# Gate and up with x stationary and the weights moving, in a two-layer GQA decode and SwiGLU kernel

## The chip, the cores and the metric

The kernel runs on one core of a Trainium2 chip. Its time is the device time of one execution, in microseconds; a profiled execution also gives a span, from the first to the last instruction, and a trace. Five engines take part: TensorE (PE; its weight loads are shown apart as PEld), VectorE (DVE), ScalarE (ACT), GpSimd (POOL) and SyncE (SP), which here issues every DMA.

## The reference

Two layers, run one after the other on the same weights. `x` is 4 rows (the batch) of 512; each layer is attention against a cache of 8192 keys and values, then a SwiGLU feed-forward:

```python
def _A_ref(x, k_cache, v_cache, wq, wo):      # 32 query heads, 8 key heads, Dh = 128
    q = (x @ wq).reshape(B, Sq, Hq, Dh).transpose(0, 2, 1, 3)
    scores = jnp.einsum("bhqd,bhkd->bhqk", q, k) * (Dh ** -0.5)
    o = jnp.einsum("bhqk,bhkd->bhqd", softmax(scores), v)
    return o.transpose(0, 2, 1, 3).reshape(B, Sq, Hq * Dh) @ wo

def _B_ref(x, w_gate, w_up, w_down):          # 512 -> 1792 -> 512
    g = _silu(x @ w_gate)
    u = x @ w_up
    return (g * u) @ w_down

for _ in range(2):
    x = x + _A_ref(_layernorm(x), A_k_cache, A_v_cache, A_wq, A_wo)
    x = x + _B_ref(_layernorm(x), B_w_gate, B_w_up, B_w_down)
```

All inputs are bfloat16. Keys and values are 4 x 8 x 8192 x 128 elements each, 64 MB each, and are read once per layer but for a few tiles that stay on the chip; w_gate, w_up and w_down have 1.8 MB each.

## The kernel before

**Slots and loads.** Keys and values come in tiles of 4 MB (one batch row, two key heads), 128 partitions of 32 KB. They go round through four slots of SBUF, with a fifth for wq and later for keys. A list `cmds` holds all loads in order; `pump` issues the next one on SP's queue as soon as the half-blocks that it writes are in `free`, and `freed` marks them free when the code reaches the last reader. SP itself then waits for that reader's semaphore. So the order of loads is fixed, and a late reader holds up every load behind it on that queue.

**Attention.** A tile of keys is turned in place on VectorE (L558), scores are matmuls with the keys moving (L582), the exponential is on ScalarE (L629), P is turned on VectorE (L646), and P times V runs in four quarters of the array: four matmuls with 32 stationary columns and 512 moving columns, each writing its own 32 PSUM partitions (L718). `gather`, `combine`, `mix` and `out_proj` bring the result back to `xT`, x with its 512 features over partitions.

**Feed-forward** (`ffn`, L943). `center` makes `xn`, the centred x, and the row sums for the variance; `deviation` (L901) is called after gate's second part and makes `rstd` with a matmul (L903) and two ScalarE operations. Gate and up (L961) hold a 128x128 block of the weight stationary and move the 4 columns of `xn` for one block of 128 features, 14 blocks by 4 contraction steps, for gate and up: 112 matmuls. The result has features over partitions, 14 groups of 4 batch columns, in one PSUM bank each for gate (`gb`) and up (`ub`). VectorE and ScalarE make `hT` from it in seven operations (L975 to L982). Parts of gate free space in layer 0: behind `wg0`, `wg1` and `wg2` come three loads of w_down, behind `wg3`, up and the w_down groups come loads of the next layer's first keys.

**w_down.** In layer 0 a 128x128 block of w_down is stationary and `hT` moves (L999), in five loads' order; in layer 1 `hT` is stationary, w_down moves 128 columns, and four quarters of the array make the four output parts (L989). `x_rows` (L879) has put x there before. The end is four small copies (L1062, L1064) and the store (L1066). All of w_up but 256 columns' worth of its last step lies in SBUF for both layers; w_gate, that rest and w_down are loaded again in layer 1, at the end of the queue. The last load, `W+`, waits until the last P has its place.

**Which feature on which partition.** The loads of w_down put e neighbouring rows on a partition (`WDS`, third number: 2 or 4), within a block of rows; `base` and `columns` pick the same features from w_gate and w_up by a stepped read, so that `hT` and w_down agree. `load_wd` is at L462.

Of the kernel before, what the change touches and what calls it, by code (L numbers as in the profile page):

```python
# [6 lines left out]
ALU = mybir.AluOpType  # L7
# [96 lines left out]
def bass_interleave_layers__gqa_block_cached__swiglu_ffn__decode_kernel(  # L104
# [12 lines left out]
    B, _, D = A_x.shape  # L117
    _, G, S, Dh = A_k_cache.shape
    HqDh = A_wq.shape[1]
    Hq = HqDh // Dh  # L120
    F = B_w_gate.shape[1]
    REP = Hq // G
    P = 128
    assert Dh == P and B * Hq == P and D % P == 0 and F % P == 0 and B == 4 and G % 2 == 0
    KT = D // P
    FO = F // P
# [5 lines left out]
    QB = 32  # L132
    NA = P // QB
# [7 lines left out]
    NSLOT = 4  # L141
# [3 lines left out]
    with ExitStack() as es:  # L145
        sb = lambda name, shape, dt: es.enter_context(nc.sbuf_tensor(name, shape, dt))

        SL = TT * Dh
# [3 lines left out]
        RES = FR * F + FY  # L152
        assert KT * HqDh == SL
        QS = NSLOT
        kvf = sb("kvf", [P, (NSLOT + 1) * SL + RES], BF16)
# [1 line left out]
        wq_sb = kv[:, QS, :].rearrange("p (k f) -> p k f", k=KT)  # L157
        WQ = [f"wq{i}" for i in range(NB)]
        wo_sb = sb("wo_sb", [P, Hq, D], BF16)
        WDS = (((12, 14, 2), (10, 12, 2), (0, 2, 2), (2, 6, 4), (6, 10, 4)), ((0, 8, 2), (8, 12, 2), (12, 14, 2)))  # L160
        NW = max(len(w) for w in WDS)

        W_SLOT = (1, 3)
        O_WU = KT * F
# [19 lines left out]
        def columns(o, e=2):  # L184
            return kvf[:, o:o + e * (P - 1) + 1:e]

        def base(L, fo):
            a, _, e = next(w for w in WDS[L] if w[0] <= fo < w[1])
            return a * P + (fo - a) // e * e * P + (fo - a) % e, e

        def wg_at(s, k, f, e):
            return columns(s * SL + k * F + f, e)

        def wu_at(s, k, f, e):
            o = k * F + f
            return columns((NSLOT + 1) * SL + o if o < RES else s * SL + O_WU + o - RES, e)

        def wd_at(s, fo, k):
            o = pick2(k).start
# [30 lines left out]
        own, rstd = tiny[:, 7:7 + QH], tiny[:, 7 + QH:7 + QH + B]  # L230
# [4 lines left out]
        xn = sb("xn", [P, XB], BF16)  # L235
# [9 lines left out]
        pb = sb("pb", [P, SW], BF16)  # L245
        pbf = pb[:].bitcast(FP32)
        acc = pbf[:, 0:Dh]
        n = FO * B
        gr, eg, gw = (pbf[:, i * n:(i + 1) * n] for i in range(3))
        hT = pb[:, 6 * n:7 * n]  # L250
# [23 lines left out]
        def bank(k):  # L274
            return ps[:, k * BANKF:(k + 1) * BANKF]
# [17 lines left out]
        def quarter(j):  # L293
# [7 lines left out]
        sem_w = {n: [sem(f"sem_{n}{i}") for i in range(c)]  # L301
                 for n, c in (("wq", 2), ("wo", 4), ("wg", 1), ("wu", 3), ("wd", NW))}
# [3 lines left out]
        def part_sem():  # L306
# [4 lines left out]
        T = _Sync(engines, prog)  # L311
# [6 lines left out]
             reads=["ident"], writes=["ident"])  # L318
        T.op("pool", lambda e: e.memset(quad[:], 0.0), writes=["quad"])
        for a in range(NA):  # L320
# [11 lines left out]
             reads=["ident"], writes=["head"])  # L332
# [3 lines left out]
             reads=["ident"], writes=["made"])  # L336
        T.op("dve", lambda e: e.tensor_reduce(sel[:].rearrange("p (h r) -> p h r", h=2),
                                              made.rearrange("p (h q r) -> p h r q", h=2, q=QH), AX.X, ALU.max),
             reads=["made"], writes=["sel"])
        T.op("dve", lambda e: e.tensor_reduce(own[:], made.rearrange("p (h q r) -> p q h r", h=2, q=QH),  # L340
                                              AX.XY, ALU.max),
             reads=["made"], writes=["own"])
# [46 lines left out]
        s = W_SLOT[0]  # L389
# [10 lines left out]
        n = NB - PARK  # L400
# [59 lines left out]
                    load_wd(w0, i, j)  # L460

        def load_wd(w0, L, j, also=()):  # L462
            a, b, e_ = WDS[L][j]
            o = 0 if w0 is pTf else wd_from(L, a)
            T.dma("sp", w0[:, o:o + (b - a) * D].rearrange("p (m x) -> p m x", x=e_ * D),
                  B_w_down[a * P:b * P, :].rearrange("(m p e) n -> p m (e n)", p=P, e=e_), sem_w["wd"][j],
                  writes=[f"wd{j}"] + list(also))

        def pump(most=len(cmds)):
# [34 lines left out]
        def freed(s, a, b):  # L504
            free.update((s, h) for h in halves(a, b))
            pump()
# [436 lines left out]
        def ffn(L):  # L943
            s = W_SLOT[L]
            gb, ub = OBK[0], SBK[0]
            gT = bank(gb)[:, 0:FO * B]
            uT = bank(ub)[:, 0:FO * B]
            fb = lambda ap: ap.rearrange("p (f b) -> p f b", b=B)
            rb = rstd[:].unsqueeze(1).to_broadcast([P, FO, B])
            rooms = {"wg0": room(s, 0, F), "wg1": room(s, F, 2 * F), "wg2": room(s, 2 * F, 3 * F), "wg3": room(s, 3 * F, O_WU), "wu0": [], "wu1": room(s, O_WU, O_WD)}  # L950
            for j, (a, b, _) in enumerate(WDS[L]):
                o = wd_from(L, a)
                rooms[f"wd{j}"] = ["pT"] if not L and a == FO_P else room(s, o, o + (b - a) * D)
            names = {"wg0": ["wg0"], "wg1": ["wg1"], "wg2": ["wg2"], "wg3": ["wg3"], "wu0": ["wu0"], "wu1": ["wu1", "wu2"]}
            for at, wname, bk, ks in ((wg_at, "wg0", gb, (0, 1)), (wg_at, "wg1", gb, (1, 2)),
                                      (wg_at, "wg2", gb, (2, 3)), (wg_at, "wg3", gb, (3, KT)),
                                      (wu_at, "wu0", ub, (0, KT // 2)), (wu_at, "wu1", ub, (KT // 2, KT))):
                for fo in range(FO):
                    f = base(L, fo)
                    for kt in range(*ks):  # L960
                        T.op("pe", lambda e: e.matmul(bank(bk)[:, fo * B:(fo + 1) * B],  # L961
                                                      lhsT=at(s, kt, *f),
                                                      rhs=xn[:, kt * B:(kt + 1) * B],
                                                      start=(kt == 0 and fo == 0), stop=(kt == KT - 1 and fo == FO - 1)),
                             reads=rooms[wname] + names[wname] + ["xn"], writes=[f"pb{bk}"],
                             sig=(fo == FO - 1 and kt == ks[1] - 1))
                if wname in ("wg0", "wg1", "wg2"):
                    k = int(wname[2])
                    if not L:
                        freed(s, NB + 2 + k, NB + 3 + k)  # L970
                    if k == 1:
                        deviation(zero_sb, "zero")
                elif wname != "wu0":
                    freed(s, *((0 if L else GATE, UP) if wname == "wg3" else (UP, DOWN)))
            T.op("dve", lambda e: e.tensor_tensor(fb(gr), fb(gT), rb, ALU.mult),  # L975
                 reads=[f"pb{gb}", "rstd"], writes=["gr", "pb"])
            T.op("act", lambda e: e.activation(eg, gr, ACTF.Exp, scale=-1.0), reads=["gr"], writes=["eg"])
            T.op("dve", lambda e: e.tensor_tensor(fb(gw), fb(gr), rb, ALU.mult), reads=["gr", "rstd"], writes=["gw"])
            T.op("dve", lambda e: e.tensor_scalar(eg, eg, 1.0, None, op0=ALU.add), reads=["eg"], writes=["eg"])
            T.op("dve", lambda e: e.reciprocal(eg, eg), reads=["eg"], writes=["eg"])  # L980
            T.op("dve", lambda e: e.tensor_tensor(eg, gw, eg, ALU.mult), reads=["gw", "eg"], writes=["eg"])
            T.op("dve", lambda e: e.tensor_tensor(hT, eg, uT, ALU.mult), reads=[f"pb{ub}", "eg"], writes=["hT"])  # L982
            if L == 1:
                x_rows(1)
                for i, (a, b, _) in enumerate(WDS[1]):
                    for fo in range(a, b):
                        for j in range(NA):
                            o = s * SL + O_WD + fo * D + j * P
                            T.op("pe", lambda e: e.matmul(quarter(j), lhsT=hT[:, fo * B:(fo + 1) * B],  # L989
                                                          rhs=kvf[:, o:o + P], start=False, stop=(fo == FO - 1)),  # L990
                                 reads=["hT", f"wd{i}"] + rooms[f"wd{i}"], writes=[f"part{j}"],
                                 sig=(fo == b - 1))
                freed(s, DOWN, NB)
                return
            for j, (a, b, _) in enumerate(WDS[0]):
                k = OBK[0] if j > WP else SBK[1]
                for nt in range(KT):
                    for fo in range(a, b):
                        T.op("pe", lambda e: e.matmul(bank(k)[:, nt * B:(nt + 1) * B],  # L999
                                                      lhsT=wd_at(s, fo, nt),  # L1000
                                                      rhs=hT[:, fo * B:(fo + 1) * B],
                                                      start=(j in (0, WP + 1) and nt == 0 and fo == a),
                                                      stop=(j in (WP, len(WDS[0]) - 1) and nt == KT - 1 and fo == b - 1)),
                             reads=["hT", f"wd{j}"] + rooms[f"wd{j}"], writes=[f"pb{k}"], sig=(fo == b - 1))
                if j == LATE[0]:
                    freed(s, DOWN, PARK)
                if j == len(WDS[0]) - 2:
                    freed(s, 0, MID)
                if j == WP:
                    add_to_x(bank(k)[:, 0:XB], f"pb{k}")  # L1010
                    freed(s, NB + 5, NB + 6)
            freed(s, MID, GATE)
            add_to_x(bank(k)[:, 0:XB], f"pb{k}")
# [82 lines left out]
```

## Time and profile before

| what | value |
|---|---|
| runs, median (lowest to highest) | 645.25 us (644.95 to 645.78) |
| profiled execution, its own time | 645.21 us |
| its span | 643.4 us |
| mean granted TensorE clock | 0.83 |
| PE / PEld / DVE / ACT / POOL busy | 65% / 28% / 66% / 7% / 2% of the span |
| DMA queue of the kernel | 271.33 MB, 99.0% of 16 engines |
| L961 (gate and up) | 224 matmuls, 7.0 us busy |
| L989 (w_down, layer 1) | 56 matmuls, 2.0 us busy |
| L999 (w_down, layer 0) | 56 matmuls, 2.3 us busy |

Busy time is a sum over the whole span; the bracket behind a row tells how long its engine was idle before it and what ended the wait. The chain of work that ended last is put down to the DMA for 61% of the span, to VectorE for 19% and to TensorE for 15%. A row "128\*4 128x128" is a matmul with 128 rows and 4 columns stationary, and 128 columns moving.

### The profile page before, as it was taken

The page shows a single profiled execution, that of the slowest core. Times are in us where ns is not written, and L with a number is a line of the kernel's source. Part 1 is how long each engine was busy: PE and PEld are TensorE (multiplying, and loading weights), DVE is VectorE, ACT ScalarE, POOL GpSimd, SP SyncE. Part 2 cuts the span into 40 slices and gives each one's busy share as a digit, 9 for nine tenths or more (in the row PEclk, how much of TensorE's full clock was granted, in tenths as well). Part 3 has the DMA queues.
Part 4 walks back from the last instruction along what each step waited for, and adds up shares of the span by engine and source line. Part 5 has one row for each costly group of instructions (what it writes and reads, how often), then busy time and mean ns, then how long its engine had stood idle before and what let it go on. Part 6 is the DMA issues. An engine that isn't in the chain of part 4 may idle for free.

```text
span 643.4 us, 7434 instructions
## 1 busy us (share of the span) xinstructions
PE 416.7 (65%) x3126; PEld 180.0 (28%) x3128; DVE 421.7 (66%) x593; ACT 42.3 (7%) x118; POOL 11.6 (2%) x44
## 2 busy tenths in 40 slices
PE   0673376456765757757866977776555577557877
PEld 0421122112222322222226432332221232222324
DVE  5275467455776656776952688887765567755964
ACT  0000000000000000000010110000000000000110
POOL 0000000000000000000000000000000000000000
PEclk9995786698877889766975899999778887769877
DMA  9999999999999999999999999999999999999996
GB/s 372 442 424 416 430 444 426 431 424 429 438 436 423 428 433 439 426 426 431 440 406 380 416 431 431 436 429 425 432 435 432 427 430 438 429 428 429 440 408 257
DMA packets 15872, 271.79 MB, mean 422 GB/s; under 512 B 1624, under 2 KB 1632, under 8 KB 7264
## 3 DMA queue, kind: packets, MB, share of 16 engines
q1 hardware_dynamic: 15840, 271.33, 99.0%
q8 instruction: 24, 0.39, 0.2%
q14 instruction: 8, 0.07, 0.0%
HBM read 271.32 MB, written 0.00 MB: 422 GB/s over the span
## 4 chain that ended last, share of the span: by engine, by line
DMA 61%; DVE 19%; PE 15%; issue 3%; another core or an unknown queue 1%; SPq 0%; DVEq 0%
DMA kvf<-in_A_k_cache_dram 49%; DVE kvf L558 15%; DMA kvf<-in_A_v_cache_dram 11%; PE ps L582 9%; PE ps L718 2%; DVE pb L770 2%; DMA kvf<-in_B_w_down_dram 1%; PE ps L961 1%; PE ps L917 1%; DVE pb L766 0%; DVE pT L646 0%; DVE scr L780 0%; SPq L93 0%; PE ps L861 0%
## 5 line engine op out<-in xcount | busy, mean ns | idle before, releaser
L582 PE MATMUL ps<-kvf,zq 128*128 128x512 bf16 x1024 | 292.9, 432 | 183.5 <-DVE kvf L558 178.8
L558 DVE STREAM_TRANSPOSE kvf<-kvf 128x2048 f32<-128x2048 f32 (+1 forms) x133 | 280.5, 2132 | 128.4 <-DMA kvf<-in_A_k_cache_dram 128.0
L582 PEld LDWEIGHTS ps<-kvf,zq 128*128 128x128 bf16 x1024 | 99.1, 108 | 340.2 <-DVE kvf L558 222.6
L718 PE MATMUL ps<-kvf,pT 128*32 128x512 bf16 x960 | 67.6, 405 | 1.1 <-DVE pT L646 1.1
L629 ACT ACTIVATE pb<-ps,tiny 128x512 bf16<-128x512 f32 x32 | 22.0, 687 | 525.9 <-DVE tiny L627 505.1
L646 DVE STREAM_TRANSPOSE pT<-pb 64x512 bf16<-64x512 bf16 x60 | 41.2, 686 | 2.7 <-ACT pb L629 1.7
L770 DVE SCALAR_TENSOR_TENSOR pb<-ps,tiny,pb 128x128 f32<-128x128 f32 x104 | 36.5, 351 | 4.7 <-PE ps L718 0.8
L588 DVE TENSOR_REDUCE tiny<-ps 128x1 f32<-128x512 f32 x32 | 22.0, 687 | 20.1 <-PE ps L582 20.1
L718 PEld LDWEIGHTS ps<-kvf,pT 128*32 128x32 bf16 x960 | 21.0, 99 | 31.2 <-issue 16.0
L775 PEld LDWEIGHTS ps<-sel,pb 128*128 128x128 f32 x64 | 17.0, 273 | 16.5 <-DVE pb L770 8.3
L572 POOL TENSOR_TENSOR zq<-scr,tiny 128x64 bf16<-128x64 bf16 x30 | 9.0, 299 | 527.1 <-PE ps L582 527.1
L596 DVE TENSOR_REDUCE mrm<-ps 1x8 f32<-1x128 f32 x32 | 8.8, 275 | 13.6 <-PE ps L593 13.6
L775 PE MATMUL ps<-sel,pb 128*128 128x8 f32 x64 | 12.4, 267 | 5.8 <-DVE pb L770 5.8
L619 PEld LDWEIGHTS ps<-mrm,tiny 128*128 128x128 f32 x60 | 13.0, 223 | 9.2 <-DVE scr L780 3.2
L917 PE MATMUL ps<-xn,kvf 128*128 128x4 bf16 x256 | 7.5, 166 | 11.5 <-DMA kvf<-in_A_wq_dram 11.2
L766 DVE TENSOR_SCALAR pb<-ps,tiny 128x128 f32<-128x128 f32 x32 | 10.1, 315 | 3.0 <-PE ps L718 3.0
L619 PE MATMUL ps<-mrm,tiny 128*128 128x16 f32 x60 | 9.9, 241 | 3.1 <-ACT mrm L631 3.1
L836 PE MATMUL ps<-wo_sb,scr 128*4 128x512 bf16 x48 | 11.0, 379 | 0.5 <-DVE scr L805 0.5
L917 PEld LDWEIGHTS ps<-xn,kvf 128*128 128x128 bf16 x256 | 7.3, 105 | 11.8 <-DMA kvf<-in_A_wq_dram 11.4
L631 ACT ACTIVATE mrm<-head,tiny 128x8 f32<-128x8 f32 x32 | 9.6, 301 | 1.0
L593 PE MATMUL ps<-identf,tiny 128*1 128x128 f32 x32 | 8.7, 273 | 0.7 <-DVE tiny L588 0.7
L790 DVE TENSOR_TENSOR xT<-xT,ps 128x16 f32<-128x16 f32 x6 | 1.0, 171 | 10.4 <-PE ps L846 4.7
(87 smaller groups left out, 120.3 us busy)
## 6 DMA issues: line engine op xcount, KB each, us to landing
kvf<-in_A_k_cache_dram SPq DMA_DIRECT2D x27, 4096.0 KB, 31.2
kvf<-in_A_v_cache_dram SPq DMA_DIRECT2D x27, 4096.0 KB, 33.9
kvf<-in_A_v_cache_dram SPq DMA_DIRECT2D x3, 2048.0 KB, 25.2
kvf<-in_A_k_cache_dram SPq DMA_DIRECT2D x9, 512.0 KB, 7.9
kvf<-in_A_k_cache_dram SPq DMA_DIRECT2D x2, 2048.0 KB, 9.4
kvf<-in_A_wq_dram SPq DMA_DIRECT2D x2, 2048.0 KB, 18.1
wo_sb<-in_A_wo_dram SPq DMA_DIRECT2D x4, 1024.0 KB, 41.4
kvf<-in_B_w_gate_dram SPq DMA_DIRECT2D x2, 1792.0 KB, 23.9
```

What stands on the lines that cost most here:

```text
L558: T.op("dve", lambda e: e.transpose(w, w), reads=names, writes=names)
L582: T.op("pe", lambda e: e.matmul(bank(bk)[:, 0:SW], lhsT=zq[:, z0:z0 + P], rhs=w[:, :, c // 2, :, c % 2], start=(q == 0 and c == 0), stop=( ...
L588: T.op("dve", lambda e: e.tensor_reduce(mx[:], bank(bk)[:, 0:SW], AX.X, ALU.max), reads=[f"pb{bk}"], writes=["mx"])
L619: T.op("pe", lambda e: e.matmul(at, lhsT=ones, rhs=mrm[:, i * H2:(i + 2) * H2], start=True, stop=True), reads=[f"m8{i}", "rsm", "onesf"], ...
L629: T.op("act", lambda e: e.activation(pb[:], bank(bk)[:, 0:SW], ACTF.Exp, bias=nm, accum_out=rs), reads=[f"pb{bk}", "nm"], writes=PB + ["rs"])
L646: T.op("dve", lambda e: e.transpose(dst, pb[hp]), reads=["pb", "row"], writes=[name])
L718: T.op("pe", lambda e: e.matmul(bank(k)[j * QB:(j + 1) * QB, q0 * Dh:q1 * Dh], lhsT=p_t[:, t, h, :], rhs=v[:, q0:q1, t, :], start=((last o ...
L766: T.op("dve", lambda e: e.tensor_scalar(into, o, own[:, q:q + 1], None, op0=ALU.mult), reads=[f"pb{k}", "own"], writes=["row"] if last els ...
L770: T.op("dve", lambda e: e.scalar_tensor_tensor(into, o, own[:, q:q + 1], into, op0=ALU.mult, op1=ALU.add), reads=[f"pb{k}", "own", iname], ...
L775: T.op("pe", lambda e: e.matmul(at, lhsT=into, rhs=sel[:], start=True, stop=True), reads=[iname, "sel"], writes=[name])
L836: T.op("pe", lambda e: e.matmul(bank(OUTB)[0:B, 0:D], lhsT=oT[:, h, :], rhs=wo_sb[:, h, :], start=(gp == groups[L][0] and r == 0), stop=(g ...
L917: T.op("pe", lambda e: e.matmul(at[:, h * B:(h + 1) * B], lhsT=wq_sb[:, kt, h * Dh:(h + 1) * Dh], rhs=xn[:, kt * B:(kt + 1) * B], start=(k ...
```

## The change

Three things change together, in both layers. Gate and up hold `xn` (4 columns) stationary and move the weight, 448 features in each quarter of the array: quarter a computes features 448a to 448a + 447, and its 4 result rows lie on partitions 32a to 32a + 3. That is 16 matmuls for gate and 17 for up, where one strip is cut at the edge of the resident part of w_up. `on_end` then turns each bank in place on VectorE, in 32x32 blocks that step over 14 features, so that feature 14p + f comes to partition p, at column b * 14 + f. The elementwise steps use that order; the last one writes `hT` back in (f, b) order. And w_down is loaded so that partition p holds rows 14p to 14p + 13: a load takes some of these 14 from every partition. The groups of w_down, their number and their order stay.

```diff
-        WDS = (((12, 14, 2), (10, 12, 2), (0, 2, 2), (2, 6, 4), (6, 10, 4)), ((0, 8, 2), (8, 12, 2), (12, 14, 2)))
+        WDS = (((12, 14), (10, 12), (0, 2), (2, 6), (6, 10)), ((0, 8), (8, 12), (12, 14)))
...
+        FW = F // NA
+        def wg_at(s, k, f, n):
+            o = s * SL + k * F + f
+            return kvf[:, o:o + n]
...
+        def strips(up, k):
+            for a in range(NA):
+                cuts = [a * FW, (a + 1) * FW]
+                if up and cuts[0] < RES - k * F < cuts[1]:
+                    cuts.insert(1, RES - k * F)
+                for f, end in zip(cuts, cuts[1:]):
+                    yield a, f, end - f
...
-            T.dma("sp", w0[:, o:o + (b - a) * D].rearrange("p (m x) -> p m x", x=e_ * D),
-                  B_w_down[a * P:b * P, :].rearrange("(m p e) n -> p m (e n)", p=P, e=e_), sem_w["wd"][j],
+            T.dma("sp", w0[:, o:o + (b - a) * D], B_w_down.rearrange("(p f) n -> p (f n)", f=FO)[:, a * D:b * D], sem_w["wd"][j],
...
+            def on_end(k):
+                blk = bank(k)[:, 0:FW].rearrange("p (i f) -> p f i", f=FO)
+                T.op("dve", lambda e: e.transpose(blk, blk), reads=[f"pb{k}"], writes=[f"pb{k}"])
...
-                for fo in range(FO):
-                    f = base(L, fo)
-                    for kt in range(*ks):
-                        T.op("pe", lambda e: e.matmul(bank(bk)[:, fo * B:(fo + 1) * B],
-                                                      lhsT=at(s, kt, *f),
-                                                      rhs=xn[:, kt * B:(kt + 1) * B],
-                                                      start=(kt == 0 and fo == 0), stop=(kt == KT - 1 and fo == FO - 1)),
+                for kt in range(*ks):
+                    parts = list(strips(bk == ub, kt))
+                    for n, (a, f, w) in enumerate(parts):
+                        T.op("pe", lambda e: e.matmul(bank(bk)[a * QB:a * QB + B, f - a * FW:f - a * FW + w],
+                                                      lhsT=xn[:, kt * B:(kt + 1) * B], rhs=at(s, kt, f, w),
+                                                      start=(kt == 0), stop=(kt == KT - 1)),
...
+            on_end(gb)
             T.op("dve", lambda e: e.tensor_tensor(fb(gr), fb(gT), rb, ALU.mult),
...
-            T.op("dve", lambda e: e.tensor_tensor(hT, eg, uT, ALU.mult), reads=[f"pb{ub}", "eg"], writes=["hT"])
+            on_end(ub)
+            T.op("dve", lambda e: e.tensor_tensor(hT.rearrange("p (f b) -> p b f", b=B), fb(eg), fb(uT), ALU.mult), reads=[f"pb{ub}", "eg"], writes=["hT"])
```

## The prediction

> **What bounds the kernel now.** I read the page, then the last 10 us in order of time, then busy time and clock by stretch, and last the same work in layer 0. The page first:
>
> ```profile
> DMA  9999999999999999999999999999999999999996
> GB/s 372 442 424 416 430 444 426 431 424 429 438 436 423 428 433 439 426 426 431 440 406 380 416 431 431 436 429 425 432 435 432 427 430 438 429 428 429 440 408 257
> ...
> q1 hardware_dynamic: 15840, 271.33, 99.0%
> ```
>
> The DMA engines are busy nearly always, so elsewhere a faster engine only waits longer for data. Two dips are to be seen: slices 21 and 22 (322 to 354 us), where layer 0 ends, and the last slice. The change touches just these: the loads around layer 0's feed-forward, and the chain that ends the kernel. That end in order of time (start, duration, engine, line):
>
> ```profile
> 635.46 0.84 PE L961 MATMUL ps<-xn,kvf 128*128 128x4 bf16 x28
> 636.13 0.30 PEld L903 LDWEIGHTS ps<-pb,tiny 128*128 128x128 f32 x2
> 636.16 0.36 PE L903 MATMUL ps<-pb,tiny 128*128 128x4 f32 x2
> 636.38 2.36 PE L961 MATMUL ps<-xn,kvf 128*128 128x4 bf16 x84
> ...
> 637.28 0.22 DVE L975 TENSOR_TENSOR pb<-ps,tiny 128x56 f32<-128x56 f32 x1 [1.47 <-PE ps L961]
> ...
> 638.58 0.22 DVE L981 TENSOR_TENSOR pb<-pb 128x56 f32<-128x56 f32 x1
> 638.90 0.21 DVE L982 TENSOR_TENSOR pb<-pb,ps 128x56 bf16<-128x56 f32 x1
> 639.16 0.74 PEld L989 LDWEIGHTS ps<-kvf,pb 128*4 128x4 bf16 x32 [0.19 <-DVE pb L982]
> ...
> 640.15 0.31 PEld L989 LDWEIGHTS ps<-kvf,pb 128*4 128x4 bf16 x16 [0.25 <-DMA kvf<-in_B_w_down_dram]
> 640.78 0.10 PEld L989 LDWEIGHTS ps<-kvf,pb 128*4 128x4 bf16 x8 [0.32 <-DMA kvf<-in_B_w_down_dram]
> 641.19 0.60 DVE L1064 CAST pb<-ps 4x128 bf16<-4x128 f32 x2 [2.08 <-PE ps L989]
> ```
>
> Two chains meet here. One is arithmetic: gate and up, SiLU on VectorE, w_down. The other is the last loads of w_down: PE twice stops for them, and the last 8 matmuls run at 640.78 because the data came then. So there is slack ahead of w_down: its 56 matmuls take less than the 2.0 us between 639.17 and 641.16. Clock and DMA in the stretches between the instants at which the clock changed:
>
> ```profile
> 629.91:633.32 3.41, 2.43 (x47) 1.21 (x41) 2.03 (x7) 0.00 (x0) 0.00 (x0) 1.00 1.01 403
> 633.32:636.74 3.42, 3.14 (x88) 2.67 (x89) 0.96 (x6) 0.18 (x1) 0.00 (x0) 1.00 0.95 354
> 636.74:640.15 3.41, 3.41 (x116) 2.95 (x112) 1.56 (x6) 0.63 (x3) 0.00 (x0) 0.50 0.37 138
> ```
>
> TensorE loses half its clock at 636.74 (third number from the end) although PE counts as fully busy: 4 moving columns a matmul are hardly any streaming.
>
> **The change part by part.**
>
> *Gate and up on TensorE.* 112 matmuls a layer (four moving columns, 28 in 0.84 us at full clock, 84 in 2.36 us mostly at half) give way to 33 with 448 moving columns (one strip is cut into 192 and 256), in four quarters. The nearest row is L718, which also writes quarters: 16 of 512 columns in 1.05 us at full clock, 24 in 2.75 us at half. With 0.38 us for the last one's own duration that is 0.22 us per round of four at full clock and 0.46 at half; for 448 columns 0.2 and 0.4. Layer 1: gate's first two rounds let the variance matmul L903 start at 635.9, where its input (L898) is ready, and not at 636.13. The deviation then comes 0.25 us sooner; gate ends at 636.7.
>
> *Two transposes a layer on VectorE.* Each is 128x448 float32 in PSUM, in place, stepping 14 elements. Rows: L558 takes 1215 ns for 1024 and 2294 ns for 2048, so 136 ns and 1.054 ns an element: 0.61 us. L521 and L524, with PSUM on one side, take 1224 and 1236 ns for 1024, the same. Bounds: 0.47 us (no fixed part), and 1.08 us if every stepped element takes two turns. I take 0.61, since L926 reads PSUM in steps of 4 elements and takes 291 ns for 128, on the unstepped rate; no row shows a stepped write. The first transpose starts at 636.73 and ends at 637.34. It covers the wait for the deviation and delays L975 from 637.28 to 637.37: +0.09. Behind it the chain to L981's end is as before. The second transpose stands alone between L981 and the last multiply, since up has long ended: 0.61 + 0.03. The last multiply writes hT in steps of 4; I cost that at nothing, as L926's stepped reading is free (0.1 us if not). w_down starts 0.73 us later, at 639.90. x_rows on PE still hides behind the second transpose.
>
> *w_down behind a later start.* All its data has landed by 640.78, and it no longer stops. Its last two rounds of four took 0.38 us; a round at half clock is a quarter of L718's 0.46, 0.11 us (L989's first 32 weight loads, eight rounds, took 0.74). 14 rounds: 12 x 0.11 + 0.38 = 1.7 us, end 641.6 against 641.16: +0.4. At full clock a round is half of that, 1.0 us in all, and the end is again set by the last load: +0.0. Which? The clock fell after a stretch with 0.12 of its time spent streaming columns (my sum over the matmul rows, by L582's 1.91 us for 8 times 512 columns, a quarter of it for a quarter of the array). It stayed up after 629.91 to 633.32 with 0.26, and fell after 616.26 to 619.67 with 0.26, so the edge is near there. Gate and part of up at 448 columns add 1.1 us to 633.32 to 636.74, 0.3 of it, so it should stay up until about 640.15 and may fall then. Five rounds at full clock and nine at half end at 641.4: **+0.25**, between the ends 0.0 and +0.5.
>
> The Trainium skill (TensorE: Matmul & The Clock Gate, What's actually happening) says the gate looks at free-running windows of about 3.4 us; the changes 3.41 us apart above agree. So where the window's edge falls varies from run to run.
>
> *Layer 0.* The clock is 0.50 throughout, so gate takes 4 x 0.4 = 1.6 us and up as much, against 3.84 us of L961. But up's second half waits for data:
>
> ```profile
> 346.24 1.00 PE L961 MATMUL ps<-xn,kvf 128*128 128x4 bf16 x28 [0.45 <-DMA kvf<-in_B_w_up_dram]
> ...
> 349.25 0.58 PE L999 MATMUL ps<-pb,kvf 128*128 128x4 bf16 x16 [0.90 <-DMA kvf<-in_B_w_down_dram]
> 350.49 0.59 PE L999 MATMUL ps<-pb,kvf 128*128 128x4 bf16 x16 [0.65 <-DMA kvf<-in_B_w_down_dram]
> ```
>
> hT comes some 0.55 us later (347.8). Three groups of 8 matmuls follow, and at 349.25 PE waited 0.90 us for w_down anyway: hidden, with 0.35 us to spare. If that cover went, 0.2 us. On SP's queue the loads of w_down behind gate are issued at about the same time; three key loads behind up and the first w_down groups some 0.5 us later. They land 5 to 9 us after issue (512 KB of keys: median 7.9 us, of which the transfer itself is 1.2 at 420 GB/s), so over 4 us of work is queued ahead of them: hidden. Cost 0.
>
> *w_down's loads.* The pieces a partition reads: layer 0 stays at 2 and 4 KB, now 14 KB apart; layer 1 goes from 2 KB to 8, 4 and 2. In 635 to 636 us, w_down's pieces run at 365 GB/s with every engine busy, against 413 in 630 to 631 with V's longer ones. 1.5 MB at the faster rate would be 0.5 us sooner: a gain's end of -0.5 on the loads, which the arithmetic above lets through only up to -0.3. Against it, the 14 KB steps; keys read in 4 KB pieces 32 KB apart run at 410 to 420 GB/s in 355 to 362, so I take 0. Loss's end: at the slowest rate of such pieces, 360 GB/s, both layers' 3.67 MB cost 1.3 us more than at 413.
>
> The Trainium skill (Perfetto Trace Analysis, DMA Optimizations) says that longer transfers, 2 KB to 4 or 8, raise throughput much. The rates just given agree in direction; by that rule the loads come 0.5 us sooner and the sum is some 645.2.
>
> Sum against the profiled execution (span 643.4, time 645.21, so 1.8 us around the span): 645.21 + 0.25 = 645.46; the median of the runs is 645.25, so **645.5 us**.
>
> **Rivals.**
> - *The clock falls to half before w_down.* For it: the window's edge is free. Then +0.4 to +0.5: 645.7. Gate and up are not the reason, since VectorE's chain ends later than up in either case.
> - *The stepped transpose is slow* (slower than before). At 1.08 us each, the first ends at 637.8 and puts L975 0.55 us back, the second adds 1.11: w_down starts at 640.8 and ends at 641.9 to 642.5, that is 646.0 to 646.6. It passes 0.2% from about 1.05 us a transpose with the clock at half. For it: both sides in PSUM and a stepped write, which no row shows. Against it: L926. The Trainium skill (SBUF — State Buffer, Door 1: The DMA port swizzle) says PSUM accesses that are not contiguous slow matmuls significantly; L926's 291 ns is against carrying that to VectorE's reads, and nothing here shows its writes.
> - *The 14 KB steps slow w_down's loads.* +0.3 to +1.3 in all, 645.8 to 646.8; layer 0's share lies on the DMA chain itself.
> - *They cure the dip at 343 to 353 us* (faster). That stretch runs at 345 to 378 GB/s against 430; all of it back is 1.3 us: 644.2 with the tail's +0.25. Against it: the pieces of layer 0 keep their size, and keys share the stretch.
> - *It does nothing*: 645.2, if w_down runs at full clock and its last load still ends it.
>
> **Numbers.** Forecast with its neighbour "does nothing" 0.39 (own range 645.1 to 645.7), clock at half 0.21, slow transpose 0.16, slow loads 0.15, fast loads 0.09. 0.2% (1.3 us) is about what a measurement of this kernel can tell from no change. Slower beyond it: rather more than half of slow transpose and of slow loads (0.18), and a seventh of the clock case, where both add up: 0.21; faster: most of fast loads, 0.07; the same: 0.72. The range leaves out a tenth on either side: 644.6 to 646.8.
>
> **What would show it.** Right: L961's successor with some 33 matmuls a layer and gate ending near 1.3 us after xn at full clock; two rows of 128x448 transposes at 0.6 us, one of them directly ahead of the last multiply; no DMA wait inside the last layer's w_down; layer 0's PE still waiting for w_down near 349. Wrong: transposes near 1 us; a w_down wait that remains (the loads are late); clock 0.50 or 1.00 through the last 4 us; a changed rate at 343 to 353.

## The result and the profile after

The changed kernel takes 647.6 us (median of 15 runs, 645.62 to 649.77), the kernel before 645.27 us (15 runs, 644.18 to 647.74). The ratio is **1.0036, 95% interval 1.0025 to 1.0046**: 2.3 us slower, outside the range of 644.6 to 646.8. The changed kernel also scatters more. The execution profiled took 648.38 us, its span is 646.6 us, so 3.17 us are to be found against the 645.21 us of before.

The page of the changed kernel first; the last rows of its second part and the third:

```profile
DMA  9999999999999999999999999999999999999995
GB/s 369 441 422 420 449 423 424 429 440 427 424 442 429 424 437 433 426 432 431 434 408 377 377 415 432 425 442 427 427 434 428 431 434 431 430 429 434 433 412 235
...
q1 hardware_dynamic: 15328, 271.33, 98.7%
q8 instruction: 23, 0.38, 0.2%
```

The same bytes move, and one slice stands out: the 23rd (about 356 to 372 us, the start of layer 1) went from 416 to 377 GB/s. The dip before it is as deep as it was. The last line was overlooked in the prediction: a second queue carries code, 16 KB a packet, and by the number and the times of its packets it is TensorE's. The kernel before had 24 such packets for 6254 matmuls and weight loads, some 260 instructions each; the kernel after has 23 for 5940.

The same place in order of time, TensorE and SyncE's issues, first in the kernel before (line numbers are eight lower there):

```profile
356.95 0.41 PE L936 MATMUL ps<-scr,identf 128*32 128x64 bf16 x16 [0.38 <-DVE scr L926]
357.71 8.38 PE L582 MATMUL ps<-kvf,zq 128*128 128x512 bf16 x32 [0.35 <-DVE zq L572]
...
370.88 1.21 SPq L93 DMA_DIRECT2D kvf<-in_A_v_cache_dram  x2
```

and in the kernel after:

```profile
357.16 0.29 PE L944 MATMUL ps<-scr,identf 128*32 128x64 bf16 x5 [0.38 <-DVE scr L934]
358.58 0.36 PE L944 MATMUL ps<-scr,identf 128*32 128x64 bf16 x11 [1.13 <-issue]
359.27 9.84 PE L590 MATMUL ps<-kvf,zq 128*128 128x512 bf16 x32 [0.33 <-DVE zq L580]
...
373.91 1.20 SPq L93 DMA_DIRECT2D kvf<-in_A_v_cache_dram  x2
```

Layer 1's 16 small matmuls that place q ran without a stop before. Now TensorE stops after the fifth for 1.13 us, and "issue" says that it waits for nothing that the profile shows. The first 32 score matmuls then take 9.84 us instead of 8.38, since the clock stays at half longer. The scores free the key slots, so SyncE's next loads go out 3.03 us later (373.91 against 370.88), and less is moved meanwhile, although the share of the DMA engines stays near full (stretches: last number GB/s, before it DMA share and granted clock; the kernel after):

```profile
364.00:366.00 2.00, 2.00 (x9) 0.82 (x8) 2.00 (x2) 0.00 (x0) 0.00 (x0) 0.80 0.89 338
366.00:368.00 2.00, 2.00 (x11) 0.87 (x10) 1.35 (x2) 0.00 (x0) 0.00 (x0) 1.00 1.06 315
368.00:370.00 2.00, 1.45 (x8) 0.51 (x6) 0.85 (x2) 0.00 (x0) 0.30 (x1) 1.00 0.97 320
```

Before, these three stretches ran at 414, 414 and 428 GB/s. By the trace's DMA records, the loads that follow land 2.1 to 3.9 us later from 381 us on, and the very last one 2.26 us later (642.99 against 640.73). That is the larger part of the 3.17 us. The rest is at the end of the kernel:

```profile
637.85 0.92 PE L973 MATMUL ps<-kvf,xn 128*4 128x448 bf16 x8
...
639.21 2.31 PE L973 MATMUL ps<-kvf,xn 128*4 128x448 bf16 x25
...
639.62 0.30 ACT L915 ACTIVATE tiny<-pb,tiny 128x4 f32<-128x4 f32 x1
...
640.18 0.67 DVE L961 STREAM_TRANSPOSE ps<-ps 128x448 f32<-128x448 f32 x1 [1.97 <-PE ps L973]
...
640.88 0.22 DVE L987 TENSOR_TENSOR pb<-ps,tiny 128x56 f32<-128x56 f32 x1
...
642.17 0.22 DVE L993 TENSOR_TENSOR pb<-pb 128x56 f32<-128x56 f32 x1
642.30 0.66 DVE L961 STREAM_TRANSPOSE ps<-ps 128x448 f32<-128x448 f32 x1
643.00 0.28 DVE L995 TENSOR_TENSOR pb<-pb,ps 128x56 bf16<-128x56 f32 x1
643.33 0.77 PEld L1002 LDWEIGHTS ps<-kvf,pb 128*4 128x4 bf16 x56 [1.77 <-DVE pb L995]
643.33 0.95 PE L1002 MATMUL ps<-kvf,pb 128*4 128x128 bf16 x56 [1.58 <-DVE pb L995]
644.38 0.60 DVE L1077 CAST pb<-ps 4x128 bf16<-4x128 f32 x2 [1.11 <-PE ps L1002]
```

w_down no longer waits for data: no DMA stands among its releasers, as was foretold. The turns take 0.67 and 0.66 us, and the second stands alone ahead of the last multiply. But the first is released by gate's last matmul at 640.18, 2.33 us after gate's first; the deviation (L915) was ready at 639.92 and covers none of it. From gate's first matmul to w_down's first it is 5.48 us; before it was 3.71. Measured against the last load, TensorE ends 1.29 us after it landed (644.28 against 642.99), and ended 0.43 us after it before (641.16 against 640.73): +0.86. With the 2.26 of the loads that makes 3.12 of the 3.17 us.

### The profile page after: what moved, and what is told of

Its sections match the earlier page's. It is cut to its first block, busy times and chain, and to the rows that moved or that the text cites. A ratio compares the mean times of both kernels' runs of the same rounds, so it can differ in the third digit from the quotient of the medians.

```text
span 646.6 us, 7122 instructions
## 1 busy us (share of the span) xinstructions
PE 413.8 (64%) x2970; PEld 173.5 (27%) x2970; DVE 424.3 (66%) x597; ACT 42.3 (7%) x118; POOL 11.6 (2%) x44
## 4 chain that ended last, share of the span: by engine, by line
DMA 61%; DVE 20%; PE 13%; issue 4%; another core or an unknown queue 1%; SPq 0%; ACT 0%; ACTq 0%; DVEq 0%
DMA kvf<-in_A_k_cache_dram 49%; DVE kvf L566 16%; DMA kvf<-in_A_v_cache_dram 11%; PE ps L590 7%; PE ps L726 2%; DVE pb L778 2%; DMA kvf<-in_B_w_down_dram 1%; PE ps L925 1%; DVE pb L774 1%; PE ps L973 0%; DVE pT L654 0%; DVE scr L788 0%; SPq L93 0%; PE ps L869 0%
## 5 line engine op out<-in xcount | busy, mean ns | idle before, releaser
L726 PE MATMUL ps<-kvf,pT 128*32 128x512 bf16 x960 | 65.8, 396 | 1.4 <-DVE pT L654 1.4
L617 DVE RECIPROCAL rl<-ps 128x8 f32<-128x8 f32 x32 | 6.5, 203 | 1.8 <-PE ps L659 1.8
```

The costliest lines, as they stand in the source:

```text
L726: T.op("pe", lambda e: e.matmul(bank(k)[j * QB:(j + 1) * QB, q0 * Dh:q1 * Dh], lhsT=p_t[:, t, h, :], rhs=v[:, q0:q1, t, :], start=((last o ...
```

## The experiments

Two causes then: a stop of TensorE at the start of layer 1, with what hangs on it (**the stop**), and VectorE's turns at the end (**the turns**). The theory of the stop: TensorE has run through one block of its code before the next has come. A change in the number of TensorE's instructions shifts where the blocks end, and in the changed kernel a block ends behind the sixth part of L944, after a block that holds hardly anything but the projection of q (128 matmuls with 128 weight loads, 4.4 us from its first matmul to L944's). The rivals: the stop comes from the new order of the loads, or from the work of the turns in layer 0.

**The same kernel, with the count restored.** The change takes 79 matmuls and 79 weight loads out of a layer's feed-forward. Here as many idle ones (a bank that is written anew later, four columns each) run at the kernel's start, where TensorE waits for data in any case. Everything else is the changed kernel.

```diff
+for _ in range(79):
+    T.op("pe", lambda e: e.matmul(bank(TOT)[:, 0:B], lhsT=ident, rhs=ident[:, 0:B], start=True, stop=True), ...)
 xb = bank_bf(OUTB)
```

> The changed kernel with 79 matmuls of 4 columns put at the very start of TensorE's program, where it waits 8 us for x; their result is not used. From layer 0's feed-forward on, TensorE's instructions stand again at the place, counted from the start of the program, where they stand in the kernel before. Theory A (TensorE waits for its code: the changed kernel's 1.4 us gap inside the 16 small matmuls of layer 1's q, which wait for nothing the profile shows, comes of where the instructions fall in 16 KB pieces of code): the gap goes from there, the keys of layer 1 start some 1.4 to 3 us sooner, and the time is 645.3 to 646.4. Theory B (the clock at the start of layer 1 only): the time stays near 647. Theory C (the w_down loads with 14 KB steps): 647 to 648, unchanged. Theory D (the two transposes at the end): unchanged.

645.85 us (12 runs) against 644.97 on the same chip, ratio 1.0013 (1.0002 to 1.0024). More work, and 1.5 us of 2.3 come back. L944 starts at 357.16 us in both, so the idle matmuls have moved nothing ahead of it, and the stop is gone:

```profile
357.16 0.41 PE L944 MATMUL ps<-scr,identf 128*32 128x64 bf16 x16 [0.38 <-DVE scr L934]
357.92 9.49 PE L590 MATMUL ps<-kvf,zq 128*128 128x512 bf16 x32 [0.35 <-DVE zq L580]
```

**The kernel before, shifted the other way.** 49 idle matmuls at the start of the kernel before put the start of layer 1 to the same place in its block as in the changed kernel: 49 and 79 are 128 pairs, 256 instructions, taken as one block (the packets gave some 260).

```diff
+for _ in range(49):
+    T.op("pe", ... the same idle matmul ...)
```

> The kernel before with 49 matmuls of 4 columns at the start of TensorE's program (98 instructions; the changed kernel has 158 fewer at the start of layer 1, and 98 = 256 - 158, so layer 1's start falls at the same place in a 16 KB piece of code of 256 instructions as in the changed kernel). Theory A: a gap of about 1.4 us appears in the small matmuls of layer 1's q, and the time rises by 1 to 2.5 us, to 646.3 to 647.8. Theories B, C and D: 645.3, as before.

647.62 us (6 runs), ratio 1.0040 (1.0028 to 1.0052). The kernel before is made as slow as the changed one by 49 matmuls in its idle start. The stop stands at its L936, one matmul further on, which bears out the 256. But a second stop came up in the last w_down, so this run cannot price the first alone:

```profile
357.15 0.30 PE L936 MATMUL ps<-scr,identf 128*32 128x64 bf16 x6 [0.38 <-DVE scr L926]
358.25 0.35 PE L936 MATMUL ps<-scr,identf 128*32 128x64 bf16 x10 [0.80 <-issue]
...
640.65 0.49 PE L989 MATMUL ps<-kvf,pb 128*4 128x128 bf16 x12
642.78 1.34 PE L989 MATMUL ps<-kvf,pb 128*4 128x128 bf16 x44 [1.64 <-issue]
```

The second stop lies behind the 112 narrow matmuls of gate and up, another long run of short instructions.

**The kernel before, shifted in layer 1 only.** With 79 more idle matmuls ahead of layer 1's eighth key strip the end of the kernel stands in its block as it did before, and only the first stop should remain.

```diff
+for _ in range(49): ...                      # at the start
 for kind, i in todo:
+    if L and (kind, i) == ("K", 8):
+        for _ in range(79): ...
```

> The kernel before with 49 idle matmuls at TensorE's start and 79 more in layer 1, ahead of its eighth key strip: 256 instructions in all. So layer 1's start stands in the 256-instruction blocks as in the changed kernel, and the end of the kernel as in the kernel before. Theory 'code': the gap at layer 1's q transposes is there (1 to 1.4 us), the loads behind it land some 2 us later, no wait for code inside the last w_down, 646.5 to 647.3, ratio 1.002 to 1.003. Rival 'the loss of the run with 49 idle matmuls came from its second wait, inside w_down': 645.0 to 645.5, ratio 1.000.

646.29 us (8 runs) against 645.12, ratio 1.0017 (1.0004 to 1.0031), a little below the range foretold. The stop is there (0.56 us of idle time in the profile), the second one is not. So by its time the kernel before is slower with the first stop alone, by some 1.1 us; the interval also holds the 1.5 us by which the 79 matmuls helped the changed kernel. Its profile does not show the way there: the last load lands at 640.92 us, 0.19 later than in the kernel before and not some 2 us, and the later start of w_down (640.33 against 639.17) goes with a clock that is at half from 631.25 us on, where it was full until 636.74 before. Nor were the 79 matmuls in layer 1 run by themselves.

**A shift by 40 instructions.** The changed kernel with 20 idle matmuls at the start.

```diff
+for _ in range(20): ...
```

> The changed kernel with 20 idle matmuls (40 instructions of TensorE) at its start, which moves the edge of the 256-instruction block from the sixth matmul of layer 1's q transposes 40 instructions back, into the dense projection of q (about 356.5 us instead of 357.2). Theory 'a block made wholly of the dense projection is run through faster than the next is fetched': the block now begins with slower work ahead of the projection, yet only 40 instructions' worth, so the wait moves with the edge and shrinks by the time that those 40 take ahead of the projection: a gap of 0 to 1 us between 356 and 357.2, and 645.8 to 647. Rival 'the place of the edge inside the transposes is what counts': no gap at all, 645.8 to 646. Rival 'the instruction place has nothing to do with it': the gap stays at the sixth transpose, 647.6.

645.94 us (11 runs), ratio 1.0014 (1.0003 to 1.0026): as good as the full 79, and no stop at all. Of the answers foretold it is the lower end of the theory's, and the rival that only the place inside the transposes counts gives the same; the rival that the place has nothing to do with it falls. The DMA records tell the two apart to some degree: the packet ahead of the stop starts at 356.12 us in the changed kernel, 3.35 us after the projection's first matmul (352.77), and TensorE goes on 1.55 us after its end. In all five stops on record TensorE goes on 1.21 to 1.55 us after the end of such a packet. With 20 idle matmuls the packet starts at 352.07, 0.57 us ahead of the projection's first matmul. So it seems to be asked for as TensorE enters the block ahead of it; when that block opens with a wait, the wait covers the fetch. That is read off packet times, and no run changed the moment of the request by itself. Nor is this moment fixed: in the five executions with 79 idle matmuls at the start, whose TensorE programs are the same up to here, the last packet ahead of the projection starts anywhere from 345.03 to 351.52 us.

**The new loads of w_down alone.** The kernel before with w_down's rows given to the partitions as in the changed kernel, and the rest untouched (so its hidden features meet the wrong rows of w_down).

```diff
-  B_w_down[a * P:b * P, :].rearrange("(m p e) n -> p m (e n)", p=P, e=e_), ...
+  B_w_down.rearrange("(p f) n -> p (f n)", f=FO)[:, a * D:b * D], ...
```

> The kernel before with only the loads of w_down changed to 14 neighbouring rows a partition, as in the changed kernel; gate and up still give the old order of features, so the rows of w_down meet other features than they should and the result is another one; the work is the same. Theory C: 646 to 647.5, with a lower rate in 343 to 353 us. Theories A, B and D: 645.0 to 645.5; with pieces of 8 KB at the end at most 0.3 us less.

644.78 us (11 runs), ratio 0.9997 (0.9988 to 1.0006). The 14 KB steps and the longer pieces cost nothing and gain nothing that can be measured (the interval reaches from -0.8 to +0.4 us).

**The turns left out.** Once from the changed kernel as it is, once with the 79 idle matmuls too.

```diff
-            on_end(gb)
-            on_end(ub)
```

> The changed kernel without its two transposes a layer; hT is then made of other elements of the banks, so the result is another one, and only VectorE's work is less. Theory D: the chain at the end is 0.7 to 1.3 us shorter and the time is 645.9 to 646.9 by that alone. Theory A: the gap inside layer 1's q matmuls stays, since TensorE's program is the same, and the time is no lower than 646.3. If layer 0's later hT were the cause of the loads being late, the gap in the loads at 362 to 380 us would go here.

> The changed kernel with the 79 idle matmuls at TensorE's start and without the two turns on VectorE (their turns are left out, so the last multiply takes gate and up unturned: the output is another). Against the run with the 79 idle matmuls alone (645.85) this is the price of the turns by themselves. Theory 'the end of the kernel pays for the second turn': 0.6 to 0.8 us less, 645.0 to 645.3, ratio to the kernel before 1.000 to 1.0005; hT comes some 0.7 us sooner after up and the last loads of w_down end the wait again. Rival 'the turns are hidden, and what is left over before is still the loads of layer 1': 645.7 to 646, as with the turns.

645.55 us (12 runs), ratio 1.0014 (1.0001 to 1.0028), and 644.94 us (11 runs), ratio 0.9993 (0.9982 to 1.0003). The first lies below both times foretold for it; its stop is still there, but lasted only 0.26 us in the profiled execution. Four kernels now form a square, each against the kernel before on its own chip:

| ratio to the kernel before | no turns | turns |
|---|---|---|
| count restored (no stop) | 0.9993 | 1.0013 |
| count as changed (stop) | 1.0014 | 1.0036 |

The turns of both layers, which no run takes apart, cost 0.0020 and 0.0022 (1.3 and 1.4 us), the stop 0.0021 and 0.0023 (1.4 and 1.5 us), and they add up. Each difference is uncertain by about 0.0015 (1 us). Without both, the kernel with gate and up in quarters and the new w_down cannot be told from the kernel before. With no turns the last w_down waits for its loads again:

```profile
638.76 0.72 PE L1000 MATMUL ps<-kvf,pb 128*4 128x128 bf16 x32
639.64 0.21 PEld L1000 LDWEIGHTS ps<-kvf,pb 128*4 128x4 bf16 x16 [0.35 <-DMA kvf<-in_B_w_down_dram]
...
640.27 0.10 PEld L1000 LDWEIGHTS ps<-kvf,pb 128*4 128x4 bf16 x8 [0.42 <-DMA kvf<-in_B_w_down_dram]
```

**One turn at a time**, with the 79 idle matmuls: first without gate's, then without up's.

```diff
-            on_end(gb)
```

> The changed kernel with the 79 idle matmuls, without the first turn (gate's; it is left out, so the output is another). Theory 'each turn stands on the path whole, as TensorE's gate ends after the deviation': hT comes 0.7 us sooner behind gate than with both turns, and some 0.7 us of the 0.9 to 1.1 us between the runs with both and with none is won: 645.1 to 645.4, ratio 1.000 to 1.0007. Rival, the prediction's step 'the first turn is covered by the wait for the deviation, and costs 0.09 us': 645.8, ratio 1.001 to 1.0013.

```diff
-            on_end(ub)
```

> The changed kernel with the 79 idle matmuls, without the second turn (up's; it is left out, so the output is another). Theory 'each turn stands on the path whole': as without the first, 0.7 us won, 645.1 to 645.4, ratio 1.000 to 1.0007; the first turn follows the end of gate and ACT's exponential waits for it. Rival, the prediction's step 'the first turn is covered': everything is won with the second alone, 644.9 to 645.1, ratio 0.9993 to 1.000, as with no turn at all.

644.77 us (12 runs), ratio 0.9993 (0.9981 to 1.0006), and 645.18 us (12 runs), ratio 1.0001 (0.9990 to 1.0012). Leaving out the first turn wins all that leaving out both wins, more than was expected of it: the prediction's step that it is covered would have left the ratio at 1.0010 to 1.0013, outside the interval. Leaving out the second wins 0.0012 of the 0.0020, by itself within the uncertainty of a difference, and between the two runs the intervals overlap. In the profile without the first turn w_down waits for its last load again, and TensorE ends 0.33 us after that load has landed:

```profile
640.56 0.10 PEld L1001 LDWEIGHTS ps<-kvf,pb 128*4 128x4 bf16 x8 [0.26 <-DMA kvf<-in_B_w_down_dram]
```

In the profile without the second it waits for no load, and TensorE ends 1.14 us after the last one:

```profile
640.65 0.95 PE L1001 MATMUL ps<-kvf,pb 128*4 128x128 bf16 x56 [0.78 <-DVE pb L994]
```

So up's turn alone fits into the slack ahead of the last loads, and both do not; that gate's turn alone would fit is not shown.

**The second turn put beside ScalarE.** With the count restored in both layers, ScalarE works 1/(1+e) by a logarithm and an exponential in place of VectorE's add and reciprocal, and up's turn comes ahead of VectorE's last but one multiply.

```diff
-  tensor_scalar(eg, eg, 1.0, None, op0=ALU.add)            # dve
-  reciprocal(eg, eg)                                       # dve
-  tensor_tensor(eg, gw, eg, ALU.mult)
-  on_end(ub)
+  activation(eg, eg, ACTF.Ln, bias=onesf[:])               # act
+  activation(eg, eg, ACTF.Exp, scale=-1.0)                 # act
+  on_end(ub)
+  tensor_tensor(eg, gw, eg, ALU.mult)
```

> The changed kernel with 79 idle matmuls at the start, 79 in layer 1 ahead of the eighth key strip, and with the sigmoid's 1/(1+e) worked by ScalarE (logarithm, then exponential) in place of VectorE's add and reciprocal; up's turn is then put ahead of VectorE's last but one multiply, so that it runs beside ScalarE. Theory: the turn leaves the path at the price of two ScalarE steps of some 0.25 to 0.5 us each against two VectorE steps, hT comes 0.3 to 0.7 us sooner than with the idle matmuls alone, 645.1 to 645.6, ratio 1.000 to 1.0008. Rival 'ScalarE has to load other tables': about 1.3 us more each time, 646.5 to 648.

645.12 us (11 runs), ratio 1.0002 (0.9993 to 1.0011). Nothing in the trace shows another table being loaded, and the turn lies beside ScalarE's 0.34 and 0.25 us:

```profile
639.52 0.34 ACT L991 ACTIVATE pb<-pb,tiny 128x56 f32<-128x56 f32 x1
639.67 0.67 DVE L961 STREAM_TRANSPOSE ps<-ps 128x448 f32<-128x448 f32 x1 [0.21 <-PE ps L973]
639.90 0.25 ACT L992 ACTIVATE pb<-pb 128x56 f32<-128x56 f32 x1
640.25 0.22 DVE L994 TENSOR_TENSOR pb<-pb 128x56 f32<-128x56 f32 x1
```

The exponential to the last multiply takes 1.26 us here (639.24 to 640.50) and 1.88 us in the kernel with 20 idle matmuls (638.22 to 640.10). That brings the changed layout level with the kernel before, not past it. In the profiled execution w_down waits for no load, but TensorE ends 0.49 us after the last one has landed (641.79 against 641.30), nearly as in the kernel before (0.43). What the second 79 matmuls do was not run apart from the move to ScalarE.

**What the stop costs depends on what else is late.** Seven of the profiled executions (idle time at the stop; duration of the 32 score matmuls behind it; issue of the V load; landing of the last load, from the DMA records):

| kernel | stop | 32 scores | V load issued | last load landed |
|---|---|---|---|---|
| before | none | 8.38 | 370.88 | 640.73 |
| after, no turns | 0.26 | 8.60 | 371.63 | 639.97 |
| after + 20 | none | 9.55 | 372.15 | 640.45 |
| before + 49 + 79 | 0.56 | 8.40 | 372.20 | 640.92 |
| after + 79 | none | 9.49 | 372.21 | 641.39 |
| before + 49 | 0.80 | 9.92 | 373.66 | 642.57 |
| after | 1.13 | 9.84 | 373.91 | 642.99 |

The five others had no stop, scores of 8.36 to 9.58 us, the V load at 370.99 to 372.25 and the last load at 640.23 to 641.30. A stop alone, or slow scores alone, move the V load by up to 1.3 us and the last load hardly beyond its own scatter of 640.0 to 641.4. Both together, in two executions, move the V load by 2.8 and 3.0 us and the last load by 1.8 and 2.3. So there seems to be slack of about 1 us in the freeing of key slots: the stop or the slow scores use it up, and where both come together the rest shows at the end. The length of the stop varies from execution to execution (0.26 and 1.13 us at the same place), and so does the moment at which the clock rises: that would explain why the changed kernel's runs lie anywhere from 645.6 to 649.8 us, though the runs that were only timed have no trace to show it.

## Why the prediction was wrong

The step that failed is **"Layer 0 ... Cost 0"** and the sum made from it: every term was a duration, and the number of TensorE's instructions was counted only for the time that they take. The feed-forward's own accounts came out nearly as written. hT comes 0.69 us later (L995 at 347.96 against L982 at 347.27; 0.55 was foretold), TensorE still waits for w_down (349.43, 0.34 us, with 0.35 foretold to be left), and x is added 0.20 us later (351.39 against 351.19), where nothing was foretold. What the step did not hold is that 158 instructions fewer shift all code behind them against the blocks in which it is fetched, and that a block then ends where nothing covers the fetch. By the square of runs the stop is worth 1.4 to 1.5 us, the larger part of the 2.3. The Trainium skill (Runtime: NRT & Kernel Launch, Instruction fetch mechanics) says that an engine's code is refilled in blocks of 16 KiB while it runs, and that crossing a block is mostly hidden; the packets of 16,384 bytes agree with the first, and the stops of 1.13 and 1.64 us are the exception to the second.

The other term that failed is **"delays L975 from 637.28 to 637.37: +0.09"**, gate's turn covered by the wait for the deviation. It rested on gate ending 1.27 us after its first matmul, at full clock. In the changed kernel's profile gate ran at half clock from the start and ended after 2.33 us, behind the deviation, so the first turn stands on the path whole; the run without it shows the same by its time. In all eight profiled executions of the changed layout gate's end releases VectorE 0.26 or 0.27 us after the deviation is ready, also where gate's first two rounds ran at full clock (with 20 idle matmuls: 637.28 against 637.01). Gate at full clock throughout was not seen. The clock case among the rivals had the right cause and the wrong consequence: it slowed only w_down, and said that gate and up "are not the reason, since VectorE's chain ends later than up in either case". That chain now begins with gate's end. w_down went the other way: its 56 matmuls ran at full clock in 0.95 us (1.0 foretold at full clock, 1.7 at half). From gate's first matmul on, w_down started 1.77 us later, not 0.73, of which gate's late end is 1.06 (2.33 against 1.27), and the end came 0.86 us later against the last load, not 0.25; beyond the term's upper end of 0.5. By the square of runs the turns are worth 1.3 to 1.4 us.

The rest, point by point:

- Gate and up: a round of four at half clock takes 0.37 us (weight loads at 639.54 and 639.91), 0.4 foretold. Right. (The row it came from, 24 matmuls in 2.75 us, gives 0.47 a round for 512 columns, not 0.46, and 0.41 for 448.)
- The turns: 0.66 to 0.67 us, 0.61 foretold. The rival of the slow turn (1.08 us) falls. The last multiply, writing in steps, takes 0.28 us instead of 0.21; nothing was foretold, with 0.1 if not.
- x_rows hides behind VectorE, w_down's data no longer holds it: right.
- The clock: the stretches shown in the prediction are steps of 3.41 us. By the trace the clock changed at 619.68, 626.50 and 636.74 us, two and three steps apart.
- w_down's loads at nothing: right, by 0.9997 with them alone. So the rival of fast strided loads falls, and that of slow ones but for its lower end (0.3 us). The Trainium skill's rule (Perfetto Trace Analysis, DMA Optimizations), that longer transfers raise the throughput much, brought nothing that can be told here; its 0.5 us lie within the interval. The dip at 343 to 353 us stayed.
- The outcome was given 0.21 for slower by over 0.2%; the mechanism behind most of it was among none of the rivals.

## What to carry to other kernels

Where a change alters how many instructions an engine has, look at the trace's packets of code beside the durations: a run of some 256 short instructions (here 4.4 us long) can end before the next block of code is there, and a handful of idle instructions in an idle place moves the edge. Ask of a step "covered by X" at both clocks that X's rival can have, because a producer that runs at half clock can become the one that ends last. And price a new wait by the slack of the loads that it holds back: here about the first 1 us cost little, and what came beyond it showed at the end.

## What was not expected of the hardware

- By all that these runs show, TensorE can stand still for its code in straight-line work: 0.26 to 1.64 us in five stops, each ending 1.21 to 1.55 us after the end of a 16 KB packet, with nothing in the profile but "issue".
- 49 idle matmuls in an idle stretch made the kernel before 0.4% slower (1.0028 to 1.0052, with two stops), and 20 idle ones made the changed kernel faster, 1.0014 against 1.0036.
- A VectorE transpose with both sides in PSUM in steps of 14 elements runs near the unstepped rate: 0.66 us for 448 elements, where the rows of before give 0.61.
